# Loading queries and keys as bf16 by casting GpSimd DMA, in one queue with the weights

## Chip, cores, metric

The kernel runs on one core of one Trainium2 chip. The metric is the device time of one execution in microseconds (us); the profile's span is 1.7 to 2.1 us shorter, as it goes from the first to the last instruction. PE is TensorE, DVE VectorE, ACT ScalarE, POOL GpSimd, SP SyncE. PSUM is the memory that TensorE writes, in banks that are reused. A *tile* is here 128 tokens; there are 36.

## The reference

```python
# q, k, v: (8, 8, 576, 64) f32;  w_in: (512, 2048), w_out: (2048, 512) f32
scores = matmul(q, k.T) / 8
ret    = matmul(scores * Dmat, v)      # Dmat[h,i,j] = gamma_h**(i-j) for i >= j, else 0
x      = ret.transpose(0, 2, 1, 3).reshape(4608, 512)
h      = x @ w_in
out    = where(h > 0, h, exp(min(h, 0)) - 1) @ w_out
```

## The kernel before

Attention is computed in chunks with a running state. Gamma factors are folded into v and into the output, so only a 0/1 mask is left. Per tile: load, cast q and k to bf16, turn them (transpose), scores, mask, product, then the FFN (the products with w_in and w_out) over groups of tiles. All loads of q, k and v stand in SyncE's queue, in the order in which they are needed; the weights are cast by GpSimd DMA. An engine runs its instructions in program order, so one that waits holds back all behind it (in run e7 below, VectorE stood 10.38 us at one cast).

```python
def load(u, after=None):                       # f32, by SyncE
    qk = raw.tile([P, 2, H, D], FP32, name="rqk", tag="rqk")
    vv = raw.tile([P, H, D], FP32, name="rv", tag="rv")
    if after is not None:
        after.memset(qk[0:1, 0, 0, 0:1], 0.0)  # a gate: the load waits for this engine
    for p0, b, s0, n in place(u):
        for dst, src in ((qk[p0:p0+n, 0], q), (qk[p0:p0+n, 1], k), (vv[p0:p0+n], v)):
            nc.sync.dma_start(dst, src[b, :, s0:s0+n, :].rearrange("h p d -> p h d"))
...
dummy(18)                  # matmuls on zeros, to raise the PE clock
cast(0, A, V); make_gx(); scale_v(0); turn(0, h); dummy(2)
for u in range(3):
    scores(u); inter(u); state(u); masks(u)
    ...                    # cast(u+1), load_w_in(0) at u == 0; the rest of the weights at u == 2
    intra(u); put_x(u); state_out(u); dummy(2)
cast(3, A, V)
for n in range(16):                        # FFN of tiles 0 to 2, 16 slots
    f1(0, n, ...)
    if n == 3:                             # a stop for tile 3
        turn(3); finish(); dummy(4, o); scores(3); masks(3); dummy(5, o)
    if n == 5: scale_v(3)
    if n == 7: product(3)
    if n == 9:
        load(4, nc.vector)
        for u in range(5, 12): load(u)
for n in range(4): f1(1, n, ...)           # FFN of tile 3
finish()
...                                        # output products, tiles 4, 5, ... in between
```

An FFN slot is `ph` (PE) -> `e` = exp (ACT) -> `m` = e - 1 (POOL) -> `g` (DVE).

Of the kernel before, what the change touches and what calls it, by code (L numbers as in the profile page):

```python
# [17 lines left out]
def kernel(  # L18
# [14 lines left out]
    P = 128  # L33
# [24 lines left out]

    const = ctx.enter_context(tc.tile_pool(name="const", bufs=1))
    raw = ctx.enter_context(tc.tile_pool(name="raw", bufs=8))  # L60
    nat = ctx.enter_context(tc.tile_pool(name="nat", bufs=5))
    tpool = ctx.enter_context(tc.tile_pool(name="tpool", bufs=4))
    ppool = ctx.enter_context(tc.tile_pool(name="ppool", bufs=3))
# [9 lines left out]
    ps_st = ctx.enter_context(tc.tile_pool(name="ps_st", bufs=1, space=PSUM))  # L73


    raws = {}

    def load(u, after=None):

        qk = raw.tile([P, 2, H, D], FP32, name="rqk", tag="rqk")  # L80
        vv = raw.tile([P, H, D], FP32, name="rv", tag="rv")
        if after is not None:
            after.memset(qk[0:1, 0, 0, 0:1], 0.0)
        for p0, b, s0, n in place(u):
            for dst, src in ((qk[p0 : p0 + n, 0], q), (qk[p0 : p0 + n, 1], k), (vv[p0 : p0 + n], v)):
                nc.sync.dma_start(dst, src[b, :, s0 : s0 + n, :].rearrange("h p d -> p h d"))  # L86
        raws[u] = (qk, vv)

    w_in_sb = const.tile([P, KJ, DF], BF16, name="w_in_sb")
    w_out_sb = const.tile([P, NFT, DM], BF16, name="w_out_sb")  # L90
# [3 lines left out]
    def load_w_in(n):  # L94
        s = slice(n * 512, (n + 1) * 512)
        nc.gpsimd.dma_start(w_in_sb[:, :, s], w_in_v[:, :, s])
# [4 lines left out]


    for u in range(4):
        load(u)

    ident = const.tile([P, P], BF16, name="ident")
    warm = const.tile([P, 512], BF16, name="warm")
    nc.vector.memset(warm, 0.0)  # L108
    scale = 1.0 / math.sqrt(D)
# [15 lines left out]
    nc.gpsimd.iota(pk_i[:, 5:9], pattern=[[P, 4]], base=64 - MID, channel_multiplier=1)  # L125
    px_i = xpool.tile([P, 2, S - 64], I32, name="px_i", tag="xt").rearrange("p a b -> p (a b)")[:, :S]
    nc.gpsimd.iota(px_i, pattern=[[1, S]], base=-MID, channel_multiplier=0)
    make_identity(nc, ident)

    mask = const.tile([P, 2, P], BF16, name="mask")  # L130
    nc.vector.memset(mask, 1.0)
    for m in range(2):
        nc.gpsimd.affine_select(
            out=mask[:, m], in_=mask[:, m], compare_op=ALU.is_ge, fill=0.0,
            base=0, pattern=[[1, P]], channel_multiplier=-1,
        )
    nc.vector.memset(mask[0:64, 1, 64:P], 0.0)

    pk = const.tile([P, R], FP32, name="pk")
    nc.vector.tensor_copy(pk, pk_i)  # L140
# [6 lines left out]
        lgk.unsqueeze(1).to_broadcast([P, R, H]),  # L147
        ALU.mult,
    )
    gk = const.tile([P, R, H], FP32, name="gk")  # L150
    nc.scalar.activation(gk, ek, AF.Exp)
    gx = const.tile([P, HP, S + 64], FP32, name="gx")

    def make_gx():
        for hp in range(HP):
            nc.scalar.activation(gx[:, hp, :S], px, AF.Exp, bias=bx, scale=lgx[:, hp : hp + 1])
        nc.gpsimd.tensor_copy(gx[:, :, S:], gx[:, :, 0:64])


    qkTs, kns, vns, scs, pts, os_, sbs, sts = {}, {}, {}, {}, {}, {}, {}, {}  # L160

    def cast(u, *engs):

        rqk, _ = raws[u]
        n = nat.tile([P, 2, H * D], BF16, name="qkn", tag="qkn")
        src = rqk.rearrange("p c h d -> p c (h d)")
        if len(engs) == 1:
            engs[0](n, src)  # L168
        else:
            for c in range(2):  # L170
                engs[c](n[:, c], src[:, c])
        kns[u] = n

    def scale_v(u):
        _, rv = raws[u]
        n = nat.tile([P, H, D], BF16, name="vn", tag="vn")
        nc.gpsimd.tensor_tensor(  # L177
            n, rv, gk[:, u % R].unsqueeze(2).to_broadcast([P, H, D]), ALU.mult
        )
        vns[u] = n  # L180

    def turn(u, bank=None):

        t = tpool.tile([P, 2, HP, P], BF16, name="qkT", tag="qkT")
        n = kns[u]
        if u < PE_TURNED:
            if bank:
                pool, tag = bank
                ps = [pool.tile([P, HP, P], BF16, name="tr", tag=tag) for c in range(2)]
            else:  # L190
                both = ps_s.tile([P, 2, 2, HP, P], BF16, name="tr", tag="sc")
                ps = [both[:, c, 0] for c in range(2)]
            for c in range(2):
                for hp in range(HP):
                    nc.tensor.transpose(ps[c][:, hp], n[:, c, hp * P : (hp + 1) * P], ident)  # L195
            nc.vector.tensor_copy(t[:, 0], ps[0])  # L196
            nc.scalar.copy(t[:, 1], ps[1])  # L197
        else:
            nc.sync.dma_start_transpose(
                t.rearrange("p c h t -> p (c h) t"), n.rearrange("p c f -> p (c f)")  # L200
            )
        qkTs[u] = t

# [13 lines left out]
    def masks(u, i=None):  # L217

        if u not in pts:
            pts[u] = ppool.tile([P, 2, HP, P], BF16, name="pt", tag="pt")  # L220
        m = mask[:, 1 if u % R == 4 else 0]
        s = slice(0, 2) if i is None else slice(i, i + 1)
        nc.vector.tensor_tensor(  # L223
            pts[u][:, s].rearrange("p i h t -> p (i h) t"), scs[u][:, s].rearrange("p i h t -> p (i h) t"),
            m.unsqueeze(1).to_broadcast([P, (s.stop - s.start) * HP, P]), ALU.mult,
        )
# [17 lines left out]
    def state(u):  # L244

        r = u % R
        if r == 8:
            return
        if r in (0, 4):
            sts[0] = ps_st.tile([P, HP, D], FP32, name="st", tag="st")  # L250
        st = sts[0]
        rows = slice(64, P) if r == 4 else slice(0, P)
        for hp in range(HP):
            for i in range(2):
                h = 2 * hp + i
                nc.tensor.matmul(  # L256
                    st[i * D : (i + 1) * D, hp], kns[u][rows, 1, h * D : (h + 1) * D], vns[u][rows, h],
                    start=(hp == 0 and r in (0, 4)), stop=(r in (3, 7)), skip_group_check=True,
                )

# [127 lines left out]
    def dummy(n, bank=(ps_m, "pm")):  # L388
        dum = bank[0].tile([P, 512], FP32, name="dum", tag=bank[1])
        for _ in range(n):  # L390
            nc.tensor.matmul(dum, warm[:, :P], warm, start=True, stop=True)  # L391

    def prep(u, *engs):
        if u < NU:
            cast(u, *engs)
            scale_v(u)

    nload = [12]

    def load_next():  # L400
        if nload[0] < NU:
            load(nload[0])
            nload[0] += 1

    def product(u):
        inter(u)
        state(u)
# [4 lines left out]
    h, m = (ps_h, "ph"), (ps_m, "pm")  # L412


    dummy(18)
    cast(0, A, V)
    make_gx()
    scale_v(0)
    turn(0, h)
    dummy(2)  # L420
    for u in range(3):
        scores(u)
        inter(u)
        state(u)
        masks(u)
        if u < 2:
            cast(u + 1, A, G)
            if u == 0:
                load_w_in(0)
            scale_v(u + 1)  # L430
            dummy(3)
            turn(u + 1, h)
        else:
            for n in range(1, 4):
                load_w_in(n)
            load_w_out(0, 0, 8)
            load_w_out(0, 8, 16)
            load_w_out(1, 0, 16)
            dummy(3)
        intra(u)  # L440
        put_x(u)
        state_out(u)
        dummy(2)
    cast(3, A, V)


    def f1(g, n, bank=None):
# [4 lines left out]
    for n in range(16):  # L452
        f1(0, n, m if n % 4 == 3 else None)
        if n == 3:
            turn(3)
            finish()
            dummy(4, o)
            scores(3)
            masks(3)
            dummy(5, o)  # L460
        if n == 5:
            scale_v(3)
        if n == 7:
            product(3)
        if n == 9:
            load(4, nc.vector)
            for u in range(5, 12):
                load(u)
    for n in range(4):
        f1(1, n, m if n == 3 else None)  # L470
    finish()
    for u, bank in enumerate((h, h, h, m)):
        ffn2_half(u, 0, bank)
    prep(4, A, G)
    ffn2_half(0, 1, h)
    turn(4)
    ffn2_half(1, 1, h)
    scores(4)
    masks(4)
    prep(5, A, G)  # L480
    ffn2_half(2, 1, h)
    product(4)
    turn(5)
    ffn2_half(3, 1, m)
    scores(5)
    masks(5)
    prep(6, A, G)
    f1(2, 0)
    f1(2, 1)
    turn(6)  # L490
    f1(2, 2)


    slots, start, now = [(f1, 2, 3, 1.0)], {}, 1.0
# [27 lines left out]
    for u in range(5, NU):  # L522
        def at(share):
            return due[u] + share * (due[u + 1] - due[u])
        events.append((due[u], 0, u))
        if u + 2 < PE_TURNED:
            events += [(due[u], -1, u + 2), (at(0.5), 1, u + 2)]
        if PE_TURNED <= u + 3 < NU:
            events.append((at(0.4) if u + 2 < PE_TURNED else due[u], -1, u + 3))
    events.sort()  # L530

    now = 0.0
    for f, g, s, d in slots:
        while events and events[0][0] <= now + d / 2:
            _, kind, u = events.pop(0)
            if kind == -1:
                prep(u, *((A, G) if u < PE_TURNED else (V,)))
                if u >= PE_TURNED:
                    turn(u)
            elif kind == 1:  # L540
                turn(u)
            else:
                load_next()
                stretch(u)
        f(g, s)
        now += d
    u = NU - 1
# [31 lines left out]
```

## Time and profile before

319.18 us (three runs, 319.08 to 319.26).

| | kernel before |
|---|---|
| PE busy, granted clock | 309.8 of 317.4 us, 0.999 |
| first transposes / first FFN matmul / first output product | 7.4 / 17.6 / 37.0 us |
| keys of tiles 0, 1, 2 landed | 5.2, 8.9, 12.5 us |
| w_in chunks 0 to 3 landed | 16.3, 22.4, 25.2, 27.8 us |

The page of the kernel before: busy time of the engines, then busy tenths in 40 slices of the span.

```profile
PE 309.8 (98%) x3020; PEld 174.7 (55%) x3020; DVE 187.8 (59%) x296; ACT 137.1 (43%) x254; POOL 145.0 (46%) x223
...
PEclk9999999999999999999999999999999999999999
DMA  8999999999999998999999767877522200000111
```

PE is the bound, and the DMA engines are full for the first half of the span. The view by stretches has, after the window, its length and the busy us of PE, PEld, DVE, ACT and POOL, then the PE clock, the DMA share and GB/s:

```profile
60.00:100.00 40.00, 39.59 (x537) 28.29 (x538) 28.87 (x43) 19.88 (x37) 22.66 (x32) 1.00 1.06 210
...
200.00:250.00 50.00, 50.00 (x435) 24.13 (x434) 32.20 (x45) 20.62 (x37) 22.23 (x32) 1.00 0.57 121
```

From 60 us on nothing is to be gained off PE. The start is different. The timeline of PE in the kernel before (start, us, what; in brackets the idle time before it and what ended it):

```profile
7.41 0.61 PE L195 MATMUL tr<-ident,qkn 128*128 128x128 bf16 x8
8.69 0.42 PE L211 MATMUL sc<-qkT 64*64 64x128 bf16 x16 [0.24 <-ACT qkT L197]
...
17.60 2.76 PE L333 MATMUL ph<-xt,w_in_sb 128*128 128x384 bf16 x16 [0.24 <-DVE xt L286]
20.20 0.61 PE L195 MATMUL tr<-ident,qkn 128*128 128x128 bf16 x8
...
24.00 2.76 PE L333 MATMUL ph<-xt,w_in_sb 128*128 128x384 bf16 x16
...
37.04 8.90 PE L374 MATMUL pmh<-w_out_sb,g 128*128 128x256 bf16 x80
45.77 0.61 PE L195 MATMUL tr<-ident,qkn 128*128 128x128 bf16 x8
```

`ph` is the FFN's first product, `pmh` the output product; at 45.77 us tile 4's transposes begin. Between 20.2 and 24.0 us tile 3 stops the FFN, mostly with dummies.

### The profile page before, as it was taken

To read this page: it belongs to the slowest core of one execution; us is meant where nothing else is said; L and a number is where in the kernel's file an instruction comes from. 1 tells how busy PE (TensorE), PEld (TensorE's weight loads), DVE (VectorE), ACT (ScalarE), POOL (GpSimd) and SP (SyncE) were. 2 spreads that over 40 slices of the span, in tenths; PEclk is the share of its full clock that TensorE was granted. 3 is DMA by queue.
4 is the path that set the end of the run, shared out by engine and by line. 5 is a ranking of instruction groups with operands and counts; after the bars stand their busy time and mean duration, and the time that the engine had idled before them with its cause. 6 is when DMAs were issued, how large, how long until landed. Compare 5 with 4: busy or idle time off the path is not lost.

```text
span 317.4 us, 7593 instructions
## 1 busy us (share of the span) xinstructions
PE 309.8 (98%) x3020; PEld 174.7 (55%) x3020; DVE 187.8 (59%) x296; ACT 137.1 (43%) x254; POOL 145.0 (46%) x223
## 2 busy tenths in 40 slices
PE   8989999999999999999999999999999999999995
PEld 3545898767766555555444444444444444444444
DVE  2765714668777777776677666666666655444300
ACT  6445524555543544344444444344444444344411
POOL 2875632555745555544554444444444433333300
PEclk9999999999999999999999999999999999999999
DMA  8999999999999998999999767877522200000111
GB/s 170 214 221 200 201 234 254 219 234 187 227 227 204 188 194 179 177 222 198 180 198 171 168 148 160 191 166 169 68 66 68 67 35 35 33 33 33 68 68 66
DMA packets 150195, 48.72 MB, mean 154 GB/s; under 512 B 138640, under 2 KB 146192, under 8 KB 150160
## 3 DMA queue, kind: packets, MB, share of 16 engines
q1 hardware_dynamic: 141888, 41.76, 66.5%
q0 software_dynamic: 6256, 4.19, 8.8%
q10 hardware_dynamic: 2016, 2.29, 2.2%
q8 instruction: 23, 0.38, 0.6%
q14 instruction: 12, 0.10, 0.1%
HBM read 36.70 MB, written 9.44 MB: 145 GB/s over the span
## 4 chain that ended last, share of the span: by engine, by line
PE 86%; DVE 4%; POOL 3%; SPq 2%; issue 2%; DMA 2%; ACT 0%; DVEq 0%; POOLq 0%
PE ph L333 36%; PE pm L358 32%; PE pmh L374 6%; PE sc L211 4%; PE o L273 3%; SPq L86 2%; PE st L256 2%; PE o L239 2%; DMA rv<-in_v_dram 2%; DVE pt L223 1%; PE tr L195 1%; DVE xt L286 1%; POOL w_out_sb L100 1%; POOL m L340 1%; DVE g L317 1%
## 5 line engine op out<-in xcount | busy, mean ns | idle before, releaser
L340 POOL TENSOR_SCALAR m<-e 128x512 bf16<-128x512 f32 (+1 forms) x156 | 93.3, 599 | 140.9 <-ACT e L338 134.1
L333 PE MATMUL ph<-xt,w_in_sb 128*128 128x512 bf16 (+3 forms) x832 | 145.6, 314 | 0.5 <-DVE xt L286 0.2
L317 DVE SCALAR_TENSOR_TENSOR g<-ph,m 128x512 bf16<-128x512 f32 (+1 forms) x156 | 100.1, 648 | 76.6 <-POOL m L340 75.2
L338 ACT ACTIVATE e<-ph 128x512 f32<-128x512 f32 (+1 forms) x156 | 88.1, 565 | 123.3 <-PE ph L333 119.5
L358 PE MATMUL pm<-w_out_sb,g 128*128 128x512 bf16 x496 | 125.5, 379 | 0.0
L333 PEld LDWEIGHTS <-w_in_sb 128*128 128x128 bf16 x832 | 71.5, 98 | 55.6 <-issue 1.5
L358 PEld LDWEIGHTS <-g 128*128 128x128 bf16 x496 | 47.9, 98 | 53.1 <-issue 0.3
L223 DVE TENSOR_TENSOR pt<-sc,mask 128x1024 bf16<-128x1024 f32 x36 | 44.0, 1221 | 10.8 <-PE sc L211 10.6
L177 POOL TENSOR_TENSOR vn<-rv,gk 128x512 bf16<-128x512 f32 x36 | 38.4, 1066 | 2.0 <-DMA rv<-in_v_dram 2.0
L286 DVE TENSOR_TENSOR xt<-o,gx 128x512 bf16<-128x512 f32 x36 | 24.7, 685 | 11.8 <-PE o L273 11.7
L365 ACT COPY ot<-pm 128x512 f32<-128x512 f32 x31 | 18.2, 587 | 14.1 <-PE pm L358 14.0
L374 PE MATMUL pmh<-w_out_sb,g 128*128 128x256 bf16 (+1 forms) x176 | 18.3, 263 | 0.0
L265 ACT CAST sb<-st 128x256 bf16<-128x256 f32 x32 | 11.9, 373 | 13.5 <-PE st L256 11.4
L211 PEld LDWEIGHTS <-qkT 64*64 64x64 bf16 x576 | 9.2, 106 | 14.9 <-issue 7.6
L374 PEld LDWEIGHTS <-g 128*128 128x128 bf16 x176 | 15.7, 98 | 1.9
L168 DVE CAST qkn<-rqk 128x1024 bf16<-128x1024 f32 x24 | 16.7, 698 | 0.0
L211 PE MATMUL sc<-qkT 64*64 64x128 bf16 x576 | 15.0, 222 | 1.5 <-ACT qkT L197 1.4
L391 PE MATMUL dum<-warm 128*128 128x512 bf16 x44 | 13.5, 442 | 1.3 <-DVE warm L108 1.3
L273 PE MATMUL o<-pt,vn 128*64 128x128 bf16 x288 | 14.4, 221 | 0.0
L379 DVE COPY oth<-pmh 128x256 f32<-128x256 f32 (+1 forms) x6 | 2.4, 401 | 18.0 <-PE pmh L374 18.0
L239 PE MATMUL o<-qkT,sb 64*64 64x128 bf16 (+1 forms) x256 | 12.3, 214 | 0.0
L197 ACT COPY qkT<-tr 128x512 bf16<-128x512 bf16 x12 | 7.0, 586 | 10.5 <-DVE qkT L196 6.9
(40 smaller groups left out, 91.2 us busy)
## 6 DMA issues: line engine op xcount, KB each, us to landing
rqk<-in_q_dram SPq DMA_DIRECT2D x32, 256.0 KB, 4.3
rqk<-in_k_dram SPq DMA_DIRECT2D x32, 256.0 KB, 4.9
rv<-in_v_dram SPq DMA_DIRECT2D x32, 256.0 KB, 4.9
out_dram<-ot SPq DMA_DIRECT2D x27, 256.0 KB, 2.3
w_in_sb<-in_moe_w_in_dram POOLq DMA_DIRECT2D x4, 512.0 KB, 8.7
out_dram<-oth ACTq DMA_DIRECT2D x9, 128.0 KB, 3.6
w_out_sb<-in_moe_w_out_dram POOLq DMA_DIRECT2D x2, 512.0 KB, 14.4
w_out_sb<-in_moe_w_out_dram POOLq DMA_DIRECT2D x1, 1024.0 KB, 22.2
```

The lines of the kernel that those rows point to most:

```text
L177: nc.gpsimd.tensor_tensor(n, rv, gk[:, u % R].unsqueeze(2).to_broadcast([P, H, D]), ALU.mult)
L211: nc.tensor.matmul(sc[j * 64 : (j + 1) * 64, i, hp], t[r, 1, hp, j * 64 : (j + 1) * 64], t[r, 0, hp], start=(hp == 0), stop=(hp == HP - 1) ...
L223: nc.vector.tensor_tensor(pts[u][:, s].rearrange("p i h t -> p (i h) t"), scs[u][:, s].rearrange("p i h t -> p (i h) t"), m.unsqueeze(1).t ...
L239: nc.tensor.matmul(o[rows, hp, :n], sbs[u][rows, hp], qkTs[u][rows, 0, hp, :n], start=(hp == 0), stop=False, skip_group_check=True,)
L273: nc.tensor.matmul(o[i * D : (i + 1) * D, hp], vns[u][:, h], pts[u][:, i, hp], start=(u % R == 0 and hp == 0), stop=(hp == HP - 1), skip_g ...
L286: nc.vector.tensor_tensor(xts[g][:, :, i * P : (i + 1) * P], os_[u], gx[:, :, s0 : s0 + P], ALU.mult)
L317: nc.vector.scalar_tensor_tensor(gt_, ph, 0.0, m, ALU.max, ALU.min)
L333: nc.tensor.matmul(ph[:, i * n : (i + 1) * n], w_in_sb[:, j, f : f + P], xts[g][:, j, :n], start=(j == 0), stop=(j == KJ - 1), skip_group_ ...
L338: nc.scalar.activation(e[:, w], ph[:, w], AF.Exp)
L340: nc.gpsimd.tensor_scalar(m[:, w], e[:, w], -1.0, 1.0, ALU.add, ALU.mult)
L358: nc.tensor.matmul(pm, gts[g, ft][:, it * P : (it + 1) * P], w_out_sb[:, ft], start=(ft == 0), stop=(ft == NFT - 1))
L374: nc.tensor.matmul(pm, gts[g, ft][:, it * P : (it + 1) * P], w_out_sb[:, ft, c0:c1], start=(ft == 0), stop=(ft == NFT - 1),)
```

## The change

The intent: no casts on the compute engines, q and k in one first-in-first-out queue with the weights, so that their order is under control, a shorter stop for tile 3, and fewer dummies. Values stay with SyncE.

```diff
-        qk = raw.tile([P, 2, H, D], FP32, name="rqk", tag="rqk")
+    def load_qk(u, *cs):
+        if u not in kns:
+            kns[u] = qkpool.tile([P, 2, H, D], BF16, name="qkn", tag="qkn")
+        for c in cs or (0, 1):
+            for p0, b, s0, n in place(u):
+                nc.gpsimd.dma_start(
+                    kns[u][p0 : p0 + n, c], (q, k)[c][b, :, s0 : s0 + n, :].rearrange("h p d -> p h d")
+                )
...
     for u in range(4):
-        load(u)
+        load_v(u)
+    load_qk(0)
...    (identity and masks: compares on DVE; load_qk(1) after the iotas)
-    dummy(18)
-    cast(0, A, V)
-    make_gx()
+    dummy(14)
+    load_qk(2)
+    make_gx(0, 1)
+    turn(0, h)
+    load_w_in(0)
     scale_v(0)
-    turn(0, h)
+    load_w_in(1)
+    scale_v(1)
+    load_qk(3)
...    (state(u) after the next tile's transposes; w_in 2, 3 and w_out at u == 0)
     for n in range(16):
         f1(0, n, m if n % 4 == 3 else None)
         if n == 3:
+            scale_v(3)
+        if n == 7:
             turn(3)
-            finish()
-            dummy(4, o)
+            load_w_out(1, 0, 16)
+            finish(1)
+            dummy(3, o)
             scores(3)
             masks(3)
-            dummy(5, o)
...
+        if n == 11:
             product(3)
-            load(4, nc.vector)
-            for u in range(5, 12):
-                load(u)
+            load_v(4, nc.vector)
+            for u in range(5, 10):
+                load_v(u)
     for n in range(4):
         f1(1, n, m if n == 3 else None)
+        if n == 1:
+            load_qk(4)
     finish()
...    (later: values and q of tile u+5, then its k, at two points of every tile's slots)
```

More of the change, by code (lines that the diff above doesn't have):

```diff
@@ L60 @@
     raw = ctx.enter_context(tc.tile_pool(name="raw", bufs=8))
+    qkpool = ctx.enter_context(tc.tile_pool(name="qkpool", bufs=8))
     nat = ctx.enter_context(tc.tile_pool(name="nat", bufs=5))
@@ L73, with load_v @@
     ps_st = ctx.enter_context(tc.tile_pool(name="ps_st", bufs=1, space=PSUM))
-    raws = {}
-    def load(u, after=None):
-        qk = raw.tile([P, 2, H, D], FP32, name="rqk", tag="rqk")
+    raws, kns = {}, {}
+    def load_v(u, after=None):
         vv = raw.tile([P, H, D], FP32, name="rv", tag="rv")
         if after is not None:
-            after.memset(qk[0:1, 0, 0, 0:1], 0.0)
+            after.memset(vv[0:1, 0, 0:1], 0.0)
         for p0, b, s0, n in place(u):
-            for dst, src in ((qk[p0 : p0 + n, 0], q), (qk[p0 : p0 + n, 1], k), (vv[p0 : p0 + n], v)):
-                nc.sync.dma_start(dst, src[b, :, s0 : s0 + n, :].rearrange("h p d -> p h d"))
-        raws[u] = (qk, vv)
+            nc.sync.dma_start(vv[p0 : p0 + n], v[b, :, s0 : s0 + n, :].rearrange("h p d -> p h d"))
+        raws[u] = vv
+    def load_qk(u, *cs):
[6 more added lines that the diff above has]
+                )
     w_in_sb = const.tile([P, KJ, DF], BF16, name="w_in_sb")
@@ L103 @@
     for u in range(4):
-        load(u)
-    ident = const.tile([P, P], BF16, name="ident")
+        load_v(u)
+    load_qk(0)
     warm = const.tile([P, 512], BF16, name="warm")
@@ L127 @@
     nc.gpsimd.iota(px_i, pattern=[[1, S]], base=-MID, channel_multiplier=0)
-    make_identity(nc, ident)
-    mask = const.tile([P, 2, P], BF16, name="mask")
-    nc.vector.memset(mask, 1.0)
-    for m in range(2):
-        nc.gpsimd.affine_select(
-            out=mask[:, m], in_=mask[:, m], compare_op=ALU.is_ge, fill=0.0,
-            base=0, pattern=[[1, P]], channel_multiplier=-1,
-        )
-    nc.vector.memset(mask[0:64, 1, 64:P], 0.0)
+    load_qk(1)
     pk = const.tile([P, R], FP32, name="pk")
@@ L149 @@
     )
+    ident = const.tile([P, P], BF16, name="ident")
+    nc.vector.tensor_scalar(ident, px[:, :P], pk[:, 0:1], None, ALU.is_equal)
+    mask = const.tile([P, 2, P], BF16, name="mask")
+    for m in range(2):
+        nc.vector.tensor_scalar(mask[:, m], px[:, :P], pk[:, 0:1], None, ALU.is_ge)
+    nc.vector.memset(mask[0:64, 1, 64:P], 0.0)
     gk = const.tile([P, R, H], FP32, name="gk")
@@ L152, with make_gx @@
     gx = const.tile([P, HP, S + 64], FP32, name="gx")
-    def make_gx():
-        for hp in range(HP):
+    def make_gx(*hps):
+        for hp in hps:
             nc.scalar.activation(gx[:, hp, :S], px, AF.Exp, bias=bx, scale=lgx[:, hp : hp + 1])
-        nc.gpsimd.tensor_copy(gx[:, :, S:], gx[:, :, 0:64])
-    qkTs, kns, vns, scs, pts, os_, sbs, sts = {}, {}, {}, {}, {}, {}, {}, {}
-    def cast(u, *engs):
-        rqk, _ = raws[u]
-        n = nat.tile([P, 2, H * D], BF16, name="qkn", tag="qkn")
-        src = rqk.rearrange("p c h d -> p c (h d)")
-        if len(engs) == 1:
-            engs[0](n, src)
-        else:
-            for c in range(2):
-                engs[c](n[:, c], src[:, c])
-        kns[u] = n
+    qkTs, vns, scs, pts, os_, sbs, sts = {}, {}, {}, {}, {}, {}, {}
     def scale_v(u):
-        _, rv = raws[u]
+        rv = raws[u]
         n = nat.tile([P, H, D], BF16, name="vn", tag="vn")
@@ L194, in turn @@
                 for hp in range(HP):
-                    nc.tensor.transpose(ps[c][:, hp], n[:, c, hp * P : (hp + 1) * P], ident)
+                    nc.tensor.transpose(ps[c][:, hp], n[:, c, 2 * hp : 2 * hp + 2].rearrange("p h d -> p (h d)"), ident)
             nc.vector.tensor_copy(t[:, 0], ps[0])
@@ L199, in turn @@
             nc.sync.dma_start_transpose(
-                t.rearrange("p c h t -> p (c h) t"), n.rearrange("p c f -> p (c f)")
+                t.rearrange("p c h t -> p (c h) t"), n.rearrange("p c h d -> p (c h d)")
             )
@@ L256, in state @@
                 nc.tensor.matmul(
-                    st[i * D : (i + 1) * D, hp], kns[u][rows, 1, h * D : (h + 1) * D], vns[u][rows, h],
+                    st[i * D : (i + 1) * D, hp], kns[u][rows, 1, h], vns[u][rows, h],
                     start=(hp == 0 and r in (0, 4)), stop=(r in (3, 7)), skip_group_check=True,
@@ L391, in dummy @@
             nc.tensor.matmul(dum, warm[:, :P], warm, start=True, stop=True)
-    def prep(u, *engs):
-        if u < NU:
-            cast(u, *engs)
-            scale_v(u)
-    nload = [12]
-    def load_next():
-        if nload[0] < NU:
-            load(nload[0])
-            nload[0] += 1
     def product(u):
@@ L423 @@
         inter(u)
-        state(u)
         masks(u)
+        if u == 0:
+            make_gx(2, 3)
         if u < 2:
-            cast(u + 1, A, G)
-            if u == 0:
-                load_w_in(0)
-            scale_v(u + 1)
             dummy(3)
@@ L433 @@
         else:
-            for n in range(1, 4):
-                load_w_in(n)
-            load_w_out(0, 0, 8)
-            load_w_out(0, 8, 16)
-            load_w_out(1, 0, 16)
-            dummy(3)
+            dummy(4)
+        state(u)
         intra(u)
@@ L443 @@
         dummy(2)
-    cast(3, A, V)
+        if u == 0:
+            scale_v(2)
+            load_w_in(2)
+            load_w_in(3)
+            load_w_out(0, 0, 8)
+            load_w_out(0, 8, 16)
     def f1(g, n, bank=None):
@@ L454 @@
         if n == 3:
+            scale_v(3)
+        if n == 7:
             turn(3)
-            finish()
-            dummy(4, o)
+            load_w_out(1, 0, 16)
+            finish(1)
+            dummy(3, o)
             scores(3)
             masks(3)
-            dummy(5, o)
-        if n == 5:
-            scale_v(3)
-        if n == 7:
+        if n == 11:
             product(3)
-        if n == 9:
-            load(4, nc.vector)
-            for u in range(5, 12):
-                load(u)
+            load_v(4, nc.vector)
+            for u in range(5, 10):
+                load_v(u)
     for n in range(4):
         f1(1, n, m if n == 3 else None)
+        if n == 1:
+            load_qk(4)
     finish()
+    scale_v(4)
+    load_qk(5)
+    nc.gpsimd.tensor_copy(gx[:, :, S:], gx[:, :, 0:64])
     for u, bank in enumerate((h, h, h, m)):
         ffn2_half(u, 0, bank)
-    prep(4, A, G)
+    scale_v(5)
+    load_qk(6)
     ffn2_half(0, 1, h)
@@ L479 @@
     masks(4)
-    prep(5, A, G)
+    scale_v(6)
+    load_qk(7)
     ffn2_half(2, 1, h)
@@ L486 @@
     masks(5)
-    prep(6, A, G)
+    load_qk(8)
     f1(2, 0)
@@ L491 @@
     f1(2, 2)
+    load_qk(9)
     slots, start, now = [(f1, 2, 3, 1.0)], {}, 1.0
@@ L526 @@
         if u + 2 < PE_TURNED:
-            events += [(due[u], -1, u + 2), (at(0.5), 1, u + 2)]
+            events += [(due[u], 3, u + 2), (at(0.5), 1, u + 2)]
         if PE_TURNED <= u + 3 < NU:
-            events.append((at(0.4) if u + 2 < PE_TURNED else due[u], -1, u + 3))
+            t = at(0.4) if u + 2 < PE_TURNED else due[u]
+            events += [(t, 1, u + 3), (t, 3, u + 3)]
+        if u + 5 < NU:
+            events += [(at(0.25), 4, u + 5), (at(0.6), 5, u + 5)]
     events.sort()
@@ L535 @@
             _, kind, u = events.pop(0)
-            if kind == -1:
-                prep(u, *((A, G) if u < PE_TURNED else (V,)))
-                if u >= PE_TURNED:
-                    turn(u)
+            if kind == 0:
+                stretch(u)
             elif kind == 1:
                 turn(u)
-            else:
-                load_next()
-                stretch(u)
+            elif kind == 3:
+                scale_v(u)
+            elif kind == 4:
+                load_v(u)
+                load_qk(u, 0)
+            else:
+                load_qk(u, 1)
         f(g, s)
```

## The prediction

> **What bounds it now.** TensorE. The page gives PE 98% busy at granted clock 0.999; the stretch view shows 49.8 to 50.0 us busy in each 50 us from 100 to 300 us, and no other engine above 73%. So the casts that leave the engines (DVE 24 x 0.70 us, ACT 12 x 0.62, POOL 10 x 0.61, by groups) are off the critical path from 60 us on. Only the start can give: PE idles 3.7 us in the first 60 us and runs 44 dummy matmuls (0.22 us each when warm). The timeline has the first transposes at 7.4 us, the first FFN matmul at 17.6, the first output-product matmul at 37.0: 19.4 us, of which real FFN work is 14; the stop for tile 3 (20.2 to 24.0) costs most of the rest.
>
> **What the change moves.** 9 fewer dummies: 2 us. Tile 3's transpose and scores come after 8 FFN slots with 3 dummies instead of 9. The cost is GpSimd: 80 casting DMAs. Its w_out issue of the same 1024 rows takes 0.91 us, so about 73 us are added to 145 busy, 7 gone again: near 70% of the span, about 85% from 60 to 100 us. An m or v scaling then waits up to 0.9 us longer. Between the end of an activation g and the reuse of its PSUM bank the 512-wide slots have 2.0 us median slack (worst 0.66), so I expect under 1 us of PE stalls in all.
>
> The Trainium skill, "DMA: Bandwidth & Descriptors", SWDGE vs HWDGE, says that casting needs the GpSimd path and that its descriptors are written by software. The trace agrees that it starts later: w_in's first packet moves 2.4 us after its issue began; q's on SyncE landed 3.3 us after issue. The first q now starts at about 3.3 us and shares the engines with four value tiles: the trace's packets show the two queues served about one for one at 34 to 38 us, and 1024 rows of 256 B take 1.2 us. Estimates: qk of tile 0 lands at 8 us (transposes 0.5 to 0.9 us later than before), tile 1 at 11.5, tile 2 at 14, w_in chunk 0 at 16.6, then 2.65 us per chunk. First FFN matmul near 18.2 (0.6 later), but from there to the first output-product matmul about 17 us instead of 19.4, as chunks 1 to 3 (19, 24, 27 us) come just in time. Net: 1.5 to 2.5 us earlier. I take a casting row to cost an engine what a 256 B copy costs (18 ns): weights cast at 41 ns per 1 KB and 81 per 2 KB, so no casting penalty shows.
>
> In the steady part each tile needs about 5 us of DMA per 7 us: enough.
>
> **Prediction: 317.0 us, range 314.0 to 320.5.** Chances: faster by over 2% 0.07, within 2% 0.83, slower by over 2% 0.10.
>
> **Signs that it is right.** First transposes 7.5 to 8.5 us; first FFN matmul 17.5 to 19; first output-product matmul 34.5 to 36; from 60 us to the end unchanged within 1 us; POOL compute near 138 us, issues of 0.9 us; DVE down about 17 us, ACT about 7.
>
> **What would make it wrong.** Slower: casting rows that write only 128 B cost more than 18 ns, so that qk or weights arrive late in the first 35 us and again at 60 to 150 us, where DMA was near saturated; or GpSimd issues take well over 0.9 us, so that m comes late and PE waits. Faster: GpSimd's queue is served before SyncE's, or cast rows are cheaper, so the start gains 4 us.

## The result and the profile after

320.19 us (four runs: 319.75, 319.88, 320.49, 320.70), against 319.22 before in the same rounds. The ratio is 1.0031, interval 1.0013 to 1.0049. The time is inside the stated range, but a gain of 0.7% was forecast and a loss of 0.3% came: the direction was wrong.

The page of the changed kernel:

```profile
PE 309.6 (97%) x3011; PEld 174.1 (55%) x3011; DVE 173.6 (55%) x272; ACT 130.7 (41%) x242; POOL 202.2 (63%) x289
...
PEclk9799999999999999999999999999999999999999
DMA  9999999997899999999999999999997200000111
```

DVE lost 14 us and ACT 6 us of work, POOL took on 57, and PE did not change. The clock has a dent in its second slice. The stretches of the changed kernel:

```profile
8.00:18.00 10.00, 8.69 (x129) 5.12 (x130) 5.17 (x8) 3.83 (x7) 9.81 (x12) 0.83 1.77 186
...
60.00:100.00 40.00, 39.68 (x517) 28.10 (x514) 27.38 (x39) 17.94 (x33) 34.08 (x45) 1.00 1.09 100
...
200.00:250.00 50.00, 50.00 (x451) 24.20 (x444) 28.89 (x39) 20.66 (x38) 31.76 (x44) 1.00 0.94 125
```

From 60 us on it is the same kernel for PE. In 8 to 18 us the clock is 0.83. The timeline of PE in the changed kernel:

```profile
7.22 0.40 PE L188 MATMUL tr<-ident,qkn 128*128 128x128 bf16 x4
9.06 0.40 PE L188 MATMUL tr<-ident,qkn 128*128 128x128 bf16 x4 [1.44 <-DMA qkn<-in_k_dram]
...
10.14 0.64 PE L204 MATMUL sc<-qkT 64*64 64x128 bf16 x16 [0.24 <-ACT qkT L190]
10.71 1.46 PE L384 MATMUL dum<-warm 128*128 128x512 bf16 x3
...
20.09 5.36 PE L326 MATMUL ph<-xt,w_in_sb 128*128 128x384 bf16 x32 [0.25 <-DVE xt L279]
25.29 0.61 PE L188 MATMUL tr<-ident,qkn 128*128 128x128 bf16 x8
...
37.62 3.66 PE L367 MATMUL pmh<-w_out_sb,g 128*128 128x256 bf16 x32
41.52 5.40 PE L367 MATMUL pmh<-w_out_sb,g 128*128 128x256 bf16 x48 [0.24 <-DVE g L310]
46.76 0.61 PE L188 MATMUL tr<-ident,qkn 128*128 128x128 bf16 x8
```

PE stands 1.44 us for the keys of tile 0, which landed at 9.02 us (5.21 before). Three dummies then take 1.46 us instead of 0.82: the trace's clock records, whose stretches are multiples of 3.41 us, grant half speed from 10.1 to 13.5 us. Such a stretch of 3.41 us at half speed is called a lost clock window below. The account against the kernel before, from these starts:

| stretch | before | after | difference |
|---|---|---|---|
| start to the first scores | 8.69 | 10.14 | +1.45 |
| first scores to first FFN matmul | 8.91 | 9.95 | +1.04 |
| first FFN matmul to first output product | 19.44 | 17.53 | -1.91 |
| first output product to tile 4's transposes | 8.73 | 9.14 | +0.41 |
| from there to the end | 271.62 | 271.82 | +0.20 |

The sum is +1.19 us, the difference of the spans (317.39 and 318.58). The third row is the gain that the change was made for. The fourth is a pause whose cause POOL's timeline shows (the changed kernel; DVE's line after it):

```profile
37.34 1.38 POOL L94 DMA_DIRECT2D qkn<-in_q_dram  x2
38.70 1.39 POOL L94 DMA_DIRECT2D qkn<-in_k_dram  x2
40.08 1.25 POOL L333 TENSOR_SCALAR m<-e 128x512 bf16<-128x512 f32 x2
...
40.77 1.29 DVE L310 SCALAR_TENSOR_TENSOR g<-ph,m 128x512 bf16<-128x512 f32 x2 [2.66 <-POOL m L333]
```

The four DMA issues in a row take 2.75 us. The third m of this FFN group starts 2.5 us after its e ended and the fourth 2.2 us after (0.08 us for the second), and g waits with them.

### The profile page after: what moved, and what is told of

It reads as the page before. It is cut to its first block, busy times and chain, and to the rows that moved or that the text cites. A ratio compares the mean times of both kernels' runs of the same rounds, so it can differ in the third digit from the quotient of the medians.

```text
span 318.6 us, 7512 instructions
## 1 busy us (share of the span) xinstructions
PE 309.6 (97%) x3011; PEld 174.1 (55%) x3011; DVE 173.6 (55%) x272; ACT 130.7 (41%) x242; POOL 202.2 (63%) x289
## 4 chain that ended last, share of the span: by engine, by line
PE 89%; DVE 4%; DMA 2%; POOL 2%; issue 1%; ACT 1%; POOLq 0%; DVEq 0%; ACTq 0%
PE ph L326 37%; PE pm L351 33%; PE pmh L367 4%; PE sc L204 4%; PE o L266 3%; PE st L249 2%; PE o L232 2%; DMA qkn<-in_k_dram 2%; PE tr L188 2%; DVE pt L216 1%; PE dum L384 1%; POOL qkn L94 1%; DVE xt L279 1%; POOL m L333 1%; DVE g L310 1%
## 5 line engine op out<-in xcount | busy, mean ns | idle before, releaser
L333 POOL TENSOR_SCALAR m<-e 128x512 bf16<-128x512 f32 (+1 forms) x156 | 91.1, 586 | 98.8 <-ACT e L331 93.5
L216 DVE TENSOR_TENSOR pt<-sc,mask 128x1024 bf16<-128x1024 f32 x36 | 44.0, 1221 | 20.8 <-PE sc L204 20.6
L170 POOL TENSOR_TENSOR vn<-rv,gk 128x512 bf16<-128x512 f32 x36 | 37.6, 1045 | 0.1
L94 POOL DMA_DIRECT2D qkn<-in_q_dram x40 | 36.1, 902 | 0.8 <-POOLq L558 0.8
L94 POOL DMA_DIRECT2D qkn<-in_k_dram x40 | 34.3, 858 | 0.1
L358 ACT COPY ot<-pm 128x512 f32<-128x512 f32 x31 | 18.2, 586 | 14.3 <-PE pm L351 14.2
L204 PEld LDWEIGHTS <-qkT 64*64 64x64 bf16 x576 | 9.4, 107 | 14.8 <-issue 10.8
L384 PE MATMUL dum<-warm 128*128 128x512 bf16 x35 | 12.4, 494 | 1.2 <-DVE warm L117 1.2
```

Source lines behind the costliest of these rows:

```text
L94: nc.gpsimd.dma_start(kns[u][p0 : p0 + n, c], (q, k)[c][b, :, s0 : s0 + n, :].rearrange("h p d -> p h d"))
L170: nc.gpsimd.tensor_tensor(n, rv, gk[:, u % R].unsqueeze(2).to_broadcast([P, H, D]), ALU.mult)
L204: nc.tensor.matmul(sc[j * 64 : (j + 1) * 64, i, hp], t[r, 1, hp, j * 64 : (j + 1) * 64], t[r, 0, hp], start=(hp == 0), stop=(hp == HP - 1) ...
L216: nc.vector.tensor_tensor(pts[u][:, s].rearrange("p i h t -> p (i h) t"), scs[u][:, s].rearrange("p i h t -> p (i h) t"), m.unsqueeze(1).t ...
L333: nc.gpsimd.tensor_scalar(m[:, w], e[:, w], -1.0, 1.0, ALU.add, ALU.mult)
```

## The experiments

All gave correct results. The first four ran on a chip on which the kernel before itself had runs of 319.06 to 325.70 us (two of them slow), so their intervals are wide (0.6%), and they are read from the traces. Two more of those runs, 323.55 and 323.59 us at a clock of 0.995, count as fast and pull the first four ratios down. Times of the parts are starts on PE; landings are from the trace's records.

| run | median us | ratio to before, interval | first FFN matmul | first output product | largest stop of PE (over 1 us) after the FFN began |
|---|---|---|---|---|---|
| changed kernel | 320.19 | 1.0031, 1.0013-1.0049 | 20.09 | 37.62 | - |
| e1_dummies | 319.75 | 0.9989, 0.9928-1.0050 | 19.32 | 36.83 | - |
| e2_tile0_sync | 325.02 | 1.0160, 1.0100-1.0219 | 17.27 | 34.79 | 5.69 at 51.9 |
| e3_v_gated | 321.63 | 1.0041, 0.9984-1.0098 | 21.73 | 39.25 | - |
| e4_qk4_late | 320.48 | 1.0016, 0.9957-1.0075 | 19.07 | 36.59 | 1.34 at 45.7 |
| e5_tile0_sync8 | 325.89 | 1.0219, 1.0191-1.0247 | 18.12 | 35.65 | 4.74 at 52.3 |
| e6_v_stagger | 326.06 | 1.0216, 1.0202-1.0229 | 23.34 | 42.54 | (5.35 at 16.4, before it) |
| e7_order_before | 328.14 | 1.0277, 1.0263-1.0291 | 17.93 | 46.49 | 8.52 at 20.7 |
| e8_stagger_qk4 | 325.37 | 1.0190, 1.0173-1.0207 | (slow profile) | | |
| e10_sync_throttle | 317.75 | 0.9951, 0.9926-0.9975 | 17.57 | 35.09 | - |
| e11_sync_throttle_late | 317.83 | 0.9948, 0.9925-0.9971 | 17.38 | 34.90 | - |
| e12_throttle_late | 319.95 | 1.0016, 0.9990-1.0042 | 20.16 | 37.68 | - |
| e13_order_only | 321.56 | 1.0050, 1.0019-1.0082 | 17.85 | 40.71 | 2.71 at 20.6 |

### More dummies (e1)

```diff
-    dummy(14)
+    dummy(21)
```

> The changed kernel with 21 instead of 14 dummy matmuls before the first transposes. They should end near 8.6 us, just before the keys of tile 0 land at 9.0, so TensorE has almost no idle time there. Theory A (the idle gap of 1.4 us costs a clock window): the clock stays at full from 6.7 us on, the stretch from the first scores to the first FFN matmul falls from 9.95 to about 8.9 us, and the time from 320.2 to about 319.2. Rival B (the late landing alone costs, the chain from the first scores is bound by VectorE and ScalarE, not by TensorE's clock): the first FFN matmul stays at 20.1 and the time within 0.3 us of the changed kernel.

The dummies did not fill the gap as meant. Here the clock was granted in full from 4.35 us (6.66 in the changed kernel's profile), so 21 dummies ended near where 14 had, and PE again stood 1.31 us for the keys. Yet this time no clock window was lost, and the stretch from the first scores to the FFN was 9.27 us instead of 9.95. So a lost window costs about 0.7 us, and it comes in some executions only: of the changed kernel's own four runs two had a mean clock of 1.000 (319.75, 319.88) and two 0.993 to 0.994 (320.70, 320.49); of e1's six, one had 0.994 (320.93). What it takes to lose one stays open: gaps of 1.4 and 1.6 us lost it in the changed kernel and e12, gaps of 1.3, 1.5 and 1.6 us did not in e1, e4 and e10. Of the two rivals both hold a part; late landing, without a lost window, still leaves 19.3 instead of 17.6.

### Tile 0 by SyncE (e2, e5)

```diff
+    rqk0 = const.tile([P, 2, H, D], FP32, name="rqk0")
+    for c in range(2):
+        nc.sync.dma_start(rqk0[:, c], (q, k)[c][0, :, 0:P, :].rearrange("h p d -> p h d"))
+    kns[0] = qkpool.tile([P, 2, H, D], BF16, name="qkn", tag="qkn")
     for u in range(4):
         load_v(u)
-    load_qk(0)
...
+    nc.scalar.copy(kns[0][:, 0], rqk0[:, 0])
+    nc.vector.tensor_copy(kns[0][:, 1], rqk0[:, 1])
     make_gx(0, 1)
```

> The changed kernel with the queries and keys of tile 0 alone loaded by SyncE as before and cast on ScalarE and VectorE; all other tiles by casting GpSimd DMA. Theory A (the late first keys, 9.0 us instead of 5.2, and the clock window lost by it are the whole loss of the start): second half of the first transposes near 7.3, first FFN matmul 17.0 to 18.0 instead of 20.1, time about 317.6 to 318.0, faster than both kernels. Rival C (the start is late because all of the early loads, the weights too, now go through one GpSimd queue): tiles 1, 2 or w_in are waited for instead, first FFN matmul stays after 19 us, time above 319.

The start did what theory A said: keys of tile 0 at 5.1 us, first FFN matmul at 17.27, first output product at 34.79 us, 2.2 us ahead of the kernel before. But the time was 325 us. PE stood 5.69 us before tile 5's scores, as ACT had not copied out the transposes: ACT itself stood at the issue of an output. In these traces the DMAs of SyncE and ScalarE carry eight completion semaphores in turn, and a DMA waits for the last user of its own; the next run asks whether two added DMAs had only shifted this pairing.

> The run that loads tile 0's queries and keys by SyncE again (e2), with the value loads of tiles 1 to 3 cut in three by heads, so that eight DMAs of the hardware queues are added instead of two. In e2 the first FFN matmul came at 17.3 us, but later ScalarE stood 9.8 us at the issue of an output, until a value load landed at 56.2; each hardware DMA waits for the eighth one before it, and two more DMAs had shifted which one that is. If that shift is the whole reason for e2's 325 us, here the output issues wait as in the changed kernel, no stop of over 1 us is seen at 50 to 60 us, the first FFN matmul is at 17.2 to 17.8, and the time is 317.2 to 318.2. If it is the casts of tile 0 or the load of the DMA engines, the stop stays and the time is above 320.

(Edit: as e2, and each value load of tiles 1 to 3 in three DMAs by heads.) The shift is not the reason: the stop stayed. ACT and PE in e5:

```profile
47.57 8.55 ACTq L379 DMA_DIRECT2D out_dram<-oth  x2
56.16 0.37 ACT L264 CAST sb<-st 128x256 bf16<-128x256 f32 x1 [8.62 <-DMA rv<-in_v_dram]
...
57.08 0.64 PE L210 MATMUL sc<-qkT 64*64 64x128 bf16 x16 [4.74 <-ACT qkT L196]
```

In the trace the output that ACT issues at 55.78 us (the second of the two in the first line) has the semaphore of a value load that was issued at 44.38 and landed at 55.71. In the changed kernel the same value load was issued at 43.22 and landed at 51.46, and the output was ready to go at 51.86: 0.4 us of slack. Starting the arithmetic 2 us earlier made the outputs due earlier while the loads got later. That points to the DMA engines as the next bound.

### Holding back values at the start (e3, e6)

```diff
-    for u in range(4):
-        load_v(u)
+    load_v(0)
     load_qk(0)
...
     nc.vector.tensor_copy(px, px_i)
+    for u in range(1, 4):
+        load_v(u, nc.vector)
```

> The changed kernel with the value loads of tiles 1 to 3 held back until VectorE has converted the positions (about 5 us), so that the first queries and keys have the DMA engines almost to themselves. If the keys of tile 0 land at 9.0 us because they share the engines with four value tiles, they land near 6.3 now, the first FFN matmul moves from 20.1 to about 18, and the time falls by about 2 us to 318.2. If it is the start of the software-written descriptors (first packet 2.6 us after issue, issues one after another) that makes them late, they land at 8.3 or later and the time falls by less than 0.8 us.

The keys landed at 6.32 us, as sharing predicts: with the engines almost to itself the casting queue is 2.7 us faster, so the late start of the software queue is only part of it. But the time did not fall. The three value loads now ran beside tile 1's keys, which landed at 11.88 us, where they had been in the changed kernel (11.75). After two gaps two clock windows were lost (half speed from 11.4 to 18.2 us). The wait had moved, not gone:

```profile
9.82 0.40 PE L189 MATMUL tr<-ident,qkn 128*128 128x128 bf16 x4 [1.08 <-DMA qkn<-in_q_dram]
11.92 0.61 PE L189 MATMUL tr<-ident,qkn 128*128 128x128 bf16 x4 [1.70 <-DMA qkn<-in_k_dram]
```

In e6 the three gates stand after the copies of tiles 0, 1 and 2's transposes.

> The changed kernel with the value loads of tiles 1, 2 and 3 each held back until the transposes of tiles 0, 1 and 2 have been copied out. e3 released all three at 5 us and only moved the delay from tile 0 to tile 1 (keys 6.3 and 11.9 us). If the values taking half of the DMA engines from the casting queue is what makes the start late, the keys land near 6.3, 8.5 and 10.5 us, the first FFN matmul comes at 16.3 to 17.3 with the clock full, and the time falls to 317.0 to 318.0. If the casting queue cannot go faster by itself, tile 1's keys land after 10 us again and the time stays above 319.5.

The keys landed at 6.1, 9.4 and 12.6 us (6.3, 8.5 and 10.5 expected), and PE lost 5.35 us later. The values of tile 2, issued at 10.07, landed at 20.48 us, beside the weights. POOL in e6:

```profile
20.62 1.04 POOL L169 TENSOR_TENSOR vn<-rv,gk 128x512 bf16<-128x512 f32 x1 [5.23 <-DMA rv<-in_v_dram]
```

The change's single queue is meant to keep queries and keys out of this; the values still meet it. The trace's packets show that the two queues are served one for one by rows, though the rows differ in size. In e2 from 14 to 16 us, 295 rows of w_in (2 KB read each) went beside 314 rows of 256 B of values: 157 value rows per us, where SyncE's queue alone started some 880 (2 to 8 us of the kernel before). Behind the weights of another queue, this load of short rows was slowed more than five times. The Trainium skill, "DMA: Bandwidth & Descriptors", section "Queues, rings and completion order", says that each DMA engine goes round its queues at packet granularity, many descriptors of one queue to a packet; the counts agree with equal turns (295 and 314 rows), but do not show how many rows make a turn.

### Tile 4's issues moved (e4, e8)

```diff
-        if n == 1:
-            load_qk(4)
+    load_qk(4)
     finish()
```

> The changed kernel with tile 4's four casting DMAs issued after the last m of the second FFN group instead of between its second and third m. In the changed kernel the third m waits 2.7 us behind these issues, VectorE's g with it, and the output products pause at 41.3 us. Expected: no pause there, tile 4 still in time, 0.3 to 0.5 us faster than the changed kernel. Rival: the pause is due to the output products' own start or the later load then stops tile 4's transposes (46.8 us), and the time does not fall.

The rival held. The pause went (first output product to tile 4's transposes 8.73 us, as before), and tile 4's keys were late instead, as their issue came later (1.5 us after the first output product began, where it was 0.3 us before it) and the DMA engines were busy with values loaded ahead (DMA share 1.53 from 38 to 48 us):

```profile
45.32 0.39 PE L188 MATMUL tr<-ident,qkn 128*128 128x128 bf16 x4
47.05 0.38 PE L188 MATMUL tr<-ident,qkn 128*128 128x128 bf16 x4 [1.34 <-DMA qkn<-in_k_dram]
```

e8 issued them earlier, on top of e6.

> e6 with tile 4's queries issued at the transposes of tile 3 and its keys after tile 3's product, where GpSimd has about 1.3 us idle each, instead of between the m's of the second FFN group. e4 only moved these issues later: the pause at 41 us went, but tile 4's keys landed at 46.9 us and its transposes waited 1.3 us. Here the keys should land before 41 us: no pause at 41 us, no wait at 44 to 47 us, 0.3 to 0.6 us faster than e6. Rival: m of the slots around tile 3 is delayed instead and nothing is gained.

Its median is 325.37 us against 326.06 of e6, but its profile fell in a slow run, so where that comes from is not told.

### The new order without the casting queue (e7, e13)

The kernel before, with the changed kernel's order at tile 3; e7 also issues w_in chunk 1 right after chunk 0.

> The kernel before, all its loads and casts, with only the changed kernel's order at tile 3: transposes and scores after 8 FFN slots with 3 dummies, product after 12, and the second w_in chunk issued right after the first. If the order alone is the gain of the change (1.9 us from the first FFN matmul to the first output product) and does not need the casting DMAs, that stretch falls from 19.4 to 17.5 us and the time from 319.2 to 317.2. Rival: w_in arrives too late in the old load order, TensorE waits for chunks 1 and 2, the stretch stays above 18.5 us and the time at 318.5 or more.

It failed in a way that I had not listed: the cast of tile 3 stands before the FFN in the programs of ACT and DVE, tile 3's keys now shared with the weights and landed at 28.2 us (19.1 before), and both engines stood at it. DVE in e7:

```profile
28.26 0.43 DVE L171 CAST qkn<-rqk 128x512 bf16<-128x512 f32 x1 [10.38 <-DMA rqk<-in_k_dram]
```

e13 keeps the old order of the weights and moves the cast to the stop:

```diff
-    cast(3, A, V)
...
-        if n == 3:
+        if n == 7:
+            cast(3, A, V)
+            scale_v(3)
             turn(3)
-            finish()
-            dummy(4, o)
+            finish(1)
+            dummy(3, o)
             scores(3)
             masks(3)
-            dummy(5, o)
...
+        if n == 11:
             product(3)
```

> The kernel before with only the order at tile 3 changed, as the changed kernel has it (after 8 FFN slots, 3 dummies instead of 9), and tile 3's cast moved there too, so that no engine stands behind its late load (in e7 ScalarE and VectorE stood at that cast until 28 us). The order of the weights is that of before. If the shorter stop is a gain of the order alone, the stretch from the first FFN matmul to the first output product falls from 19.4 to 17.5 us and the time to 317.2. If the second w_in chunk, which landed at 22.4 us in the kernel before, then sets the pace, TensorE waits about 2 us for it near 20.3, the stretch stays at 19 us or more and the time at 319.0 to 320.5: then the gain needs the weights that the one casting queue brings earlier (18.1 us).

PE in e13:

```profile
23.34 4.38 PE L333 MATMUL ph<-xt,w_in_sb 128*128 128x384 bf16 x16 [2.71 <-DMA w_in_sb<-in_moe_w_in_dram]
28.87 0.62 PE L195 MATMUL tr<-ident,qkn 128*128 128x128 bf16 x8 [1.15 <-ACT qkn L171]
```

The second chunk landed at 23.3 us and set the pace, and a clock window went too. The stretch was 22.9 us: the 17.5 hoped for, the wait of 2.71, another of 1.15 for tile 3's cast (an effect of moving it to the stop), and about 1.6 for the half clock. The wait for w_in alone is more than the 1.9 us to be gained. The three runs that lost no window (clock 0.998 to 1.000) took 320.0 to 320.7 us, still longer than before. So in the kernel before the stop for tile 3 was no waste: it covered the wait for w_in. In this load order the gain of 1.9 us does need the weights earlier, which the one casting queue gives (chunk 1 at 18.05 us).

### Later values held back (e10, e11, e12)

Theory D, by now: up to about 57 us the DMA engines are the limit, and values of tiles 6 to 9, loaded far ahead, delay what is needed now.

```diff
-            for u in range(5, 10):
-                load_v(u)
+            load_v(5)
...
     finish()
+    load_v(6, nc.vector)
...
     turn(4)
+    load_v(7, nc.vector)
...
     turn(5)
+    load_v(8, nc.vector)
...
     turn(6)
+    load_v(9, nc.vector)
```

e10 is e2 with this edit, e11 adds e4's, e12 is e4 with this edit alone.

> e2 (tile 0's queries and keys by SyncE) with the value loads of tiles 6 to 9 held back to VectorE's work on the second FFN group and on tiles 4, 5 and 6, instead of all being issued at 30 us. Theory D: from 0 to 57 us the DMA engines are the limit; in e2 and e5 a start 2 us earlier was lost again because ScalarE's seventh output waits for the semaphore of a value load that was issued at 44 us and landed only at 56, behind loads that nobody needs yet. With those held back no stop of over 1 us is seen at 50 to 60 us, the first output product is at 34.8, and the time is 317.0 to 317.8, faster than both kernels. Rival: the stop comes from the casting queue or the outputs themselves; then it stays at 4 us or more and the time above 321.

> e10 with tile 4's casting DMAs after the last m of the second FFN group (as e4). e4 gained nothing as tile 4's keys then landed at 46.9 us. If that was the load of the DMA engines, here both the pause of 0.4 us and the wait for tile 4's keys are absent, and the time is 0.3 to 0.6 us under e10, 316.5 to 317.3. If the keys are late by their own issue, a wait of 1 us or more stays before tile 4's transposes and the time is that of e10 or longer.

> e4 (the changed kernel, tile 4's casting DMAs later) with the value loads of tiles 6 to 9 held back in the same way; tile 0 stays with GpSimd. Theory D: tile 4's keys land before 44 us, the wait of 1.3 us before its transposes is gone, and the time falls from 320.2 (e4) to 318.7 to 319.2 when no clock window is lost. Rival: no change from e4.

e10 and e11 are faster than the kernel before: 317.75 and 317.83 us, ratios 0.9951 and 0.9948, both intervals below 1. (The changed kernel did not run in those rounds; in its own it was slower than the kernel before.) The stop is gone. PE in e2, then in e10 at the same place:

```profile
57.58 0.64 PE L207 MATMUL sc<-qkT 64*64 64x128 bf16 x16 [5.69 <-ACT qkT L193]
```

```profile
49.87 1.91 PE L370 MATMUL pmh<-w_out_sb,g 128*128 128x256 bf16 x16
51.70 0.42 PE L207 MATMUL sc<-qkT 64*64 64x128 bf16 x16
```

In e11 neither the pause nor the wait for tile 4 is left. Its span, 314.9 us, is 0.6 under e10's (315.5), but the medians are level, and the 316.5 to 317.3 us expected did not come: six runs of each go from 317.1 to 318.4 us at a clock of 0.998 or more. What spreads them is open. In e12 the wait of 1.34 us before tile 4 is gone too (first output product to tile 4's transposes 8.73 us). Its one run with a clock of 1.000 took 318.85 us, as expected; the five others, at 0.989 to 0.994, 319.50 to 321.12 us, as tile 0 still comes late there.

The pairs e2 and e10, e4 and e12 differ in nothing but the gates. The second shows what theory D says: tile 4's last keys were issued 21.0 us after the first FFN matmul in both, and landed 27.8 us after it in e4, 25.4 in e12. The first shows that loading tiles 6 to 9 ahead makes the stop, but two things changed with the gates. Loads landed sooner (tile 6's keys 5.2 us after their issue, 11.4 in e2), and ScalarE's seventh output now follows another load on its semaphore (one that landed at 43.43 us, 5.9 before the output; in e2 one that landed at 56.21, just before it). No run tells these two apart.

## Why the prediction was wrong

- *TensorE is the bound and the casts are off its path from 60 us on.* Right as far as the profile can say: PE's busy time from 60 to 300 us is 239.34 us before and 239.44 after, though DVE lost 13.5 us there. No run took the casts away alone.
- *GpSimd issues of 0.91 us, under 1 us of PE stalls.* Right: the groups give 902 and 858 ns for q and k, 70 us in all, and the stall was 0.41 us. But an m waited 2.5 us, not up to 0.9: the stall came from four issues in a row at 37 us, not from the steady part.
- *A casting row costs an engine what a copy costs (18 ns).* No penalty in rate: almost alone, from 10 to 12 us, the casting queue started 2165 such rows in 2 us, 14.8 ns per engine and row. (One row's own record lasts 32 ns in the median, 18 for a 256 B copy; the records overlap, with a DMA share of 2.32 in that window.)
- *The stretch from the first FFN matmul to the first output product shrinks to 17 us.* Nearly: 17.53. The reason given, weights just in time, holds, and e13 shows that it is needed.
- *First FFN matmul near 18.2 (0.6 later).* This is the step that failed: 20.09, 2.5 us later, more than the 1.9 us gained. Its terms: tile 0's keys landed at 9.0 instead of 8 us (the first issue began at 1.26 us, the first packet moved at 3.9, not 3.3; from there to the landing took 5.1 us, where four lots of 1024 rows at the 1.2 us of the prediction come to 4.8, an estimate), and the first scores came 1.45 us later. And I took the chain from the first scores to the FFN as long as before, 8.9 us. It took 9.95. About 0.7 us of that is a clock window lost after PE's wait (9.27 in e1, 9.28 in e4, without a loss), which the prediction did not have at all. The other 0.3 us was not tested; e1 and e4, which keep it, waited 0.53 us for tile 1's keys.
- *In the steady part each tile needs 5 us of DMA per 7 us: enough.* True of the steady part (PE is busy for 50.0 of 50 us from 200 to 250 us), but the first 57 us were not costed as a budget. e2 and e5 show what that hid: even with the start mended, the prefetch ate the gain and more.

## What to carry to other kernels

Before moving a load to another queue, cost the first tens of microseconds as a DMA budget: here two queues shared the engines row by row, so 256 B rows beside rows of 2 KB fell from some 880 to 157 per us. Load the first operand by the path that starts soonest (tile 0's keys landed at 5.1 us by SyncE, at 9.0 by GpSimd), keep what can wait behind a gate, and look which engine's program holds an instruction that waits for such a load. Idle gaps in front of the first matmuls cost their own length and sometimes a clock window on top (0.7 us here).

## What the Trainium skill lacked or had wrong

- "DMA: Bandwidth & Descriptors" gives about 1 us to the first byte for DMAs issued from GpSimd (Specifications; Latency and other measured facts). Here the first q's issue ran from 1.26 to 2.35 us and its first packet moved at 3.9 us: 2.6 us from the start of the issue, 1.6 us from its end.
- The same page's Specifications ask for at least 512 B for line rate and tell of a read-modify-write below it. 128 B cast rows moved at 14.8 ns per engine and row here, and 256 B copies of SyncE's queue alone at 18 ns (some 880 rows per us on 16 engines); it gives no figure for casting rows.
- The same page (Queues, rings and completion order) has the round-robin, but not what it does to a queue of short rows: 157 rows per us beside w_in, 880 alone.
- "TensorE: Matmul & The Clock Gate", Part 1, in its table of the two states, lets the clock fall after at least one idle window of about 3.4 us. Here half speed was granted for 3.41 us after a window (6.66 to 10.08 us) in which PE was idle for only 1.8 us in all, 1.44 of it in one gap (changed kernel); gaps of 1.3 and 1.5 us did not cost it (e1, e4). The window's length agrees.
- No page that I read tells that an output DMA of ACT can share its completion semaphore with a load of SyncE and stand for it (e5: from 47.91 to 55.78 us, with ACT idle for 8.6 us).
